# An RWKV recurrence with a cosine feed-forward on one core: block 1's own products earlier, its states later, the least value inside the scan, and weights' high parts on GpSimd

## The chip, the cores and the metric

The kernel runs on one core of a Trainium2 chip. The metric is the device time of one execution in microseconds, lower is better; the time shown is the median of the runs. In the text PE is TensorE, DVE is VectorE, ACT is ScalarE, POOL is GpSimd and SP is SyncE, which issues the DMAs.

## The reference

Per batch (4) and head (8), over 768 steps with 48 channels, a state of 48x48 decays by `w` and takes in `k v`; the output of all heads goes through a feed-forward of 384 to 2048 to 384 with `h*cos(h)`:

```python
for t in range(S):
    kt, vt, rt, wt = k[:, :, t], v[:, :, t], r[:, :, t], w[:, :, t]
    cur = np.einsum('bhd,bhe->bhde', u[None] * kt, vt)
    y[:, :, t] = np.einsum('bhd,bhde->bhe', rt, state + cur)
    state = wt[:, :, :, None] * state + np.einsum('bhd,bhe->bhde', kt, vt)
...
h = x @ w_in
g = h * np.cos(h)
return g @ w_out
```

## The kernel before, in words

The 3072 tokens are cut into 24 chunks of 128 tokens (4 batches, 6 chunks each), and two chunks make a block of 256 tokens. Chunk numbers `j` run through the batches first, so chunks 0 to 3 are the first of their batches and have no past state. The 2048 hidden channels are 16 weight tiles `w0` to `w15` of 128 channels, which stay in SBUF once they are prepared.

Attention of a chunk is a row of steps, named as in the tables that set the order:
- `load`, `lv`, `lr`: DMAs of `tt` (r, k and decays), `v`, and from chunk 8 on `rk`.
- `decay` (att_decay, L201): in the first eight chunks the product `rkt` (L205); a scan backwards over the decays into `ee` (L208), which gives the decay from each token to the end of the chunk; a lower bound on the whole decay (L212), its reciprocal (L213), a scan forwards (L214), and the scaled r (`r3`, L218) and k (`k3`, L219).
- `diag`: a product with `u` (a matmul `pc` in the first eight chunks, L230 to L233 on DVE after that), spread to a diagonal matrix `asb` by POOL (L237).
- `a`: scores `pa` on PE (L260), taken under a mask into `asb` by DVE (L262). `o` (L301): a block's own products `py` (L315, L320). `t`: transposed keys `kn`. `s`: states `pst` and `sn`. `d`: the decayed state `dd` and its copies `past`. `p` (L323): the products with the past (L330, L334), and the block's output `xT` split into a high and a low part.

The feed-forward of a block takes eight units of two weight tiles each. `mm1` (L383) makes `ph` in PSUM with three products per tile: high by high, high by low, low by high. The gate (L354) goes ACT L358, DVE L359, ACT L360, DVE L361, then ACT casts the high part `gs` (L141) and POOL subtracts it in two halves (L144) for the low part. `mm2` (L402) multiplies by the second matrix into `acc`. The first 16 units take turns between blocks 0 and 1 (`PAIR`), so that each weight tile serves twice while the next ones are prepared.

A weight tile arrives as packed bits (`raw`) and is rebuilt by `load_weights` (L153): three ACT passes (L163, L166, L167), a shift and an addition on DVE (L168, L169), the cast to the high part (`whi0`, a copy, L141: on ACT before) and the subtraction that gives the low part (`wlo0`, L144, on DVE).

What sets the order: the strings `START` (L61) and `PLAN` (L53) are PE's order, written out by hand ("w" prepares a weight tile and "f" fetches one, "m0 m1" are the halves of an mm1, a digit is a chunk or block). All other engines are ordered by a scheduling layer. `att` (L438) pulls in what a step needs, and forces older steps first where buffers run out. `EARLY` and `LATER` name the engine of each step: EARLY holds while START runs, which covers the attention of chunks 0 to 5, LATER from then on. The PSUM banks of `ph` are two while both blocks are under way, so an mm1 waits for the last gate step (L361) of the unit two before it.

```python
        if i < 2:
            stage[0] = 1 if i else 2
```

Of the kernel before, what the change touches and what calls it, by code (L numbers as in the profile page):

```python
# [17 lines left out]
ALU = mybir.AluOpType  # L18
# [19 lines left out]
LEAST = 1e-15  # L38
# [6 lines left out]

LAG = 3
HP = 50
EARLY = dict(rkt="v", cd="a", pc0="a", pc1="a", wadd="v", wm="a", whi0="a", whi1="a", ksh="a", gh="a", xh="a", rzh0="p", rzh1="v", r3="v", k3="v", rk="p", ru="p", rf0="v", rf1="v", kn="a", dd="v", rd0="a", rd1="a", rz0="v", rz1="v", ks="v", g0="p", g1="p", x="v", wlo0="v", wlo1="p", qf="s", qt="s", qr="s", qv="s", qx0="s", qx1="s", qo="s")
LATER = dict(pc0="a", pc1="a", ksh="v", gh="a", xh="a", rzh0="a", rzh1="a", r3="p", k3="v", rk="v", ru="v", rf0="v", rf1="v", kn="v", dd="v", rz0="v", rz1="v", ks="p", g0="p", g1="p", x="v", qf="s", qt="s", qr="s", qv="s", qx0="s", qx1="a", qo="s")
OFF = 0  # L50
FLEAD = 1
LEAD = 0
# [6 lines left out]
        "mm1 mm2 decay+5",  # L59
        "mm1 d+5 mm2 lr+6"]  # L60
START = ["load0 load1 f lv0 decay0 f diag0 a0 lv1 decay1 diag1 a1 w load2 f w o0 x0 decay2 diag2 m0 m1",  # L61
# [4 lines left out]
PAIR = "0001110101010101"  # L66
# [5 lines left out]
def rwkv_cos_ffn(ctx: ExitStack, tc: tile.TileContext, tr, tn, tv, u, ut, wts, w, rkw, vst, us, xs, out):  # L72
    nc = tc.nc
# [23 lines left out]
    def buf(tag, shape, dtype, name=None, pool=sb):  # L97
        return pool.tile(shape, dtype, tag=tag, name=name or tag, bufs=BUFS.get(tag, 1))
# [6 lines left out]
    mask = cst.tile([C, 4, C], U8, name="mask")  # L105
    nc.vector.tensor_copy(out=mask, in_=maskf)
    one_e = cst.tile([R, NP, 129], F32, name="one_e")
    nc.vector.memset(one_e, 0.0)
    nc.vector.memset(one_e[:, :, 128:129], 1.0)
    inj = cst.tile([R, NP, 129], F32, name="inj")  # L110
    nc.vector.memset(inj, 0.0)
# [5 lines left out]
    wholes = cst.tile([R, NG, NP], F32, name="wholes")  # L117
# [13 lines left out]
    def engines(codes):  # L131
        E.update({k: {"v": nc.vector, "p": nc.gpsimd, "a": nc.scalar, "s": nc.sync}[e] for k, e in codes.items()})
# [7 lines left out]
    def copy(name, out, in_):  # L140
        (nc.scalar.copy if E[name] is nc.scalar else E[name].tensor_copy)(out=out, in_=in_)  # L141
# [32 lines left out]
    NB = NG // NCB  # L174
# [4 lines left out]
    def att_load(j):  # L179
        a = atts[j] = {"j": j}  # L180
        a["g"] = g = order[j]
        a["b"], a["c"] = divmod(g, NCB)
        a["tt"] = tt = buf("tt", [R, TRW], F32)
        for cols in ((1024, TRW), (512, 1024), (0, 512)) if j < IN_PARTS else ((0, TRW),):
            E["qt"].dma_start(out=tt[:, slice(*cols)], in_=tr[g, :, slice(*cols)])
        a["r3"] = tt[:, 0:512].rearrange("p (a t) -> p a t", a=NP)
        a["k3"] = tt[:, 512:1024].rearrange("p (a t) -> p a t", a=NP)
        if j == 0:
            E["qt"].dma_start(out=u_by_head, in_=ut)
        if j == BY_PE:  # L190
            E["qt"].dma_start(out=u_sb, in_=u.to_broadcast([C, DM]))
# [9 lines left out]
    def att_decay(a):  # L201

        if a["j"] < BY_PE:
            a["rkt"] = buf("rkt", [R, NP, C], F32)
            E["rkt"].tensor_tensor(out=a["rkt"], in0=a["r3"], in1=a["k3"], op=ALU.mult)  # L205
        wp = a["tt"][:, 1024:1024 + W129 + 1]
        a["ee"] = ee = buf("ee", [R, NP, 129], F32)
        nc.vector.tensor_tensor_scan(out=ee.rearrange("p a t -> p (a t)")[:, ::-1], data0=wp[:, 1:W129 + 1][:, ::-1],  # L208
                                     data1=one_e.rearrange("p a t -> p (a t)")[:, ::-1],
                                     initial=0.0, op0=ALU.mult, op1=ALU.add)  # L210
        whole = wholes[:, a["j"]]
        nc.vector.tensor_single_scalar(out=whole, in_=ee[:, :, 0], scalar=LEAST, op=ALU.max)  # L212
        nc.vector.reciprocal(out=inj[:, :, 0], in_=whole)  # L213
        nc.vector.tensor_tensor_scan(out=wp[:, 0:W129], data0=wp[:, 0:W129], data1=inj.rearrange("p a t -> p (a t)"),  # L214
                                     initial=0.0, op0=ALU.mult, op1=ALU.add)
        pp = wp[:, 0:W129].rearrange("p (a t) -> p a t", a=NP)
        a["pp"] = pp[:, :, 0:C]
        E["r3"].tensor_tensor(out=a["r3"], in0=a["r3"], in1=a["pp"], op=ALU.mult)  # L218
        E["k3"].tensor_tensor(out=a["k3"], in0=a["k3"], in1=ee[:, :, 1:129], op=ALU.mult)  # L219
# [150 lines left out]
    def mm1(t, part=None):  # L370
        i, u = seq[t]
        if not part:
            weights("f", (u + 1) * FU + LEAD + FLEAD)
            weights("w", (u + 1) * FU + LEAD)
            for j in range(BLK):
                att(i * BLK + j, "x")
            units[t] = bank("h", [C, FU, BT], "ph")
        xT, ph = xts[i], units[t]
        for fi in range(FU) if part is None else (part,):
            n = 0  # L380
            for kt in range(KT):
                for a, b in PASSES:
                    nc.tensor.matmul(out=ph[:, fi], lhsT=wgt[u * FU + fi][:, 0, a, kt * 128:(kt + 1) * 128], rhs=xT[:, b, kt],  # L383
                                     start=n == 0, stop=n == 3 * KT - 1)
                    n += 1
        if part is None or part == FU - 1:
            units[t] = gate(sb, ph)
# [39 lines left out]
    for i in PAIR:  # L427
# [5 lines left out]
    n_checked = [0]  # L433
    done = {"f": 0, "w": 0}
    steps = dict(load=None, lr=att_load_rk, lv=att_load_v, decay=att_decay, diag=att_diag, d=att_dstate,
                 a=att_scores, t=att_transpose, s=att_state, o=att_own, p=att_past, x=att_x)

    def att(j, n):  # L438

        whole = n in "osp"  # L440
        if not 0 <= j < (NBLK if whole else NG) or (j, n) in seen:
            return
        for m in ("decay" if n == "diag" and j < BY_PE else NEEDS.get(n, "")).split():
            for c in (range(j * BLK, (j + 1) * BLK) if whole and m not in "osp" else (j,)):
                att(c, m)
        i = j // BLK
        if n == "load":
            for m in "osp":
                att((j - BUFS["tt"]) // BLK, m)
        elif n == "t":  # L450
            att((j - BUFS["kn"]) // BLK, "s")
        elif n == "d":
            att(i - SAME, "s")
            att((j - BUFS["dd"]) // BLK, "s")
            att(i - 1, "p")
        elif n == "lv":
            att((j - BUFS["v"]) // BLK, "o")
            att((j - BUFS["v"]) // BLK, "s")
        elif n == "x":
            att(i, "p")  # L460
        seen.add((j, n))
        if n == "load":
            att_load(j)
        else:
            steps[n](j if whole else atts[j])
# [19 lines left out]
    def events(i, row, t=None):  # L485
        for e in row.split():
            if e == "mm1":
                if t is not None:
                    up(0)
            elif e == "mm2":  # L490
                if t is not None and up1[1] <= t - LAG:
                    up(1)
            else:
                n, _, d = e.partition("+")
                att(i * (1 if n in "osp" else BLK) + int(d), n)
# [211 lines left out]
```

## Time and profile before

| | |
|---|---|
| time, median of 3 runs (lowest, highest) | 551.72 us (550.91, 552.66) |
| the profiled execution: own time, span | 554.87 us, 553.1 us |
| busy: PE, DVE, ACT, POOL | 517.9, 364.2, 270.5, 215.7 us |
| DMA | 51.38 MB, mean 93 GB/s |

Busy time is the union of an engine's instructions over the span, so a high share can hide a stage in which the engine waits. In the timeline a row has start, duration, engine, source line, operation, tiles with shapes and how many were merged; in brackets the idle time ahead of it and who ended it. A row of the waits has the total, the number of times and the longest. Start to start of two rows on PE is the better measure of a group of matmuls, since their ends overlap.

### The profile page before, as it was taken

The numbers are of one execution on the slowest core, as the hardware profiler recorded it, in microseconds if no ns is written. First come the engines' busy times: TensorE is split into PE (matmuls) and PEld (weight loads), VectorE is DVE, ScalarE is ACT, GpSimd is POOL, SyncE is SP. The second block draws the span as 40 slices with busy tenths as digits, with TensorE's granted clock in tenths as the row PEclk, the third lists the DMA queues.
The fourth block names the chain that finished last, engine by engine and source line by source line (L and its number), as shares of the span: only waits on it lengthen the run. The fifth ranks groups of instructions, "written<-read, shape, count | busy, mean of one in ns | idle before, by whom it ended". The sixth has DMA issues, their size and how long they took to land. (4 is left out here: it accounts for less than half of the span.)

```text
span 553.1 us, 11951 instructions
## 1 busy us (share of the span) xinstructions
PE 517.9 (94%) x4980; PEld 491.9 (89%) x4980; DVE 364.2 (66%) x574; ACT 270.5 (49%) x456; POOL 215.7 (39%) x268
## 2 busy tenths in 40 slices
PE   4656999989998999999999999999999999999996
PEld 3555999879998999999999999999999999999995
DVE  7999999955869468468468468468469674433321
ACT  1879998335424434434434435334443254444542
POOL 2151166623525335335335336335334334323332
PEclk9956899989999999999999999999999999999998
DMA  8985842005352043042042042043033340000000
GB/s 280 337 269 179 249 133 94 29 3 134 99 154 56 17 127 79 19 135 69 21 134 69 20 147 56 22 125 74 6 96 128 115 144 1 30 1 1 30 2 31
DMA packets 16440, 51.38 MB, mean 93 GB/s; under 512 B 1984, under 2 KB 8384, under 8 KB 16384
## 3 DMA queue, kind: packets, MB, share of 16 engines
q1 hardware_dynamic: 16240, 50.49, 30.2%
q8 instruction: 40, 0.66, 0.5%
q14 instruction: 16, 0.13, 0.1%
q10 hardware_dynamic: 144, 0.10, 0.1%
HBM read 45.87 MB, written 4.72 MB: 91 GB/s over the span
## 5 line engine op out<-in xcount | busy, mean ns | idle before, releaser
L144 POOL TENSOR_TENSOR gs<-rr,gs 128x256 fp32r<-128x256 f32 x192 | 156.2, 834 | 258.1 <-ACT gs L141 233.1
L383 PE MATMUL ph<-xT,w 128*128 128x256 f32 x1728 | 224.6, 285 | 6.4 <-DVE rr L361 3.5
L402 PE MATMUL acc<-w,gs 128*128 128x384 f32 x1152 | 222.1, 342 | 5.0 <-DVE asb L262 2.8
L383 PEld LDWEIGHTS ph<-xT,w 128*128 128x128 f32 x1728 | 215.5, 192 | 10.5 <-DVE w L144 2.9
L402 PEld LDWEIGHTS acc<-w,gs 128*128 128x128 f32 x1152 | 197.4, 190 | 11.0 <-DVE asb L262 3.5
L360 ACT ACTIVATE rr<-rr,quarter 128x512 f32<-128x512 f32 x96 | 69.5, 724 | 117.0 <-DVE rr L359 117.0
L359 DVE SCALAR_TENSOR_TENSOR rr<-rr,ph 128x512 f32<-128x512 int32 x96 | 65.6, 683 | 81.2 <-ACT rr L358 67.7
L361 DVE TENSOR_TENSOR rr<-rr,ph 128x512 f32<-128x512 f32 x96 | 65.3, 680 | 47.2 <-ACT rr L360 47.2
L358 ACT ACTIVATE rr<-ph 128x512 int32<-128x512 f32 x96 | 57.0, 593 | 57.0 <-PE ph L383 56.9
L141 ACT CAST gs<-rr 128x512 fp32r<-128x512 f32 x96 | 59.0, 615 | 51.7 <-PE acc L402 40.0
L237 POOL TENSOR_SCALAR_AFFINE_SELECT asb<-cd 128x512 f32<-128x512 f32 x48 | 34.3, 747 | 43.0 <-PE py L320 23.3
L262 DVE COPY_PREDICATED asb<-mask,pa 128x512 f32<-128x512 uint8 x48 | 32.7, 735 | 5.3 <-PE pa L260 5.3
L218 POOL TENSOR_TENSOR tt<-tt 112x512 f32<-112x512 f32 x18 | 23.6, 1309 | 28.3 <-DVE tt L214 27.1
L260 PE MATMUL pa<-tt 48*128 48x128 f32 x384 | 32.0, 311 | 2.3 <-DVE tt L219 2.2
L208 DVE TENSOR_TENSOR_SCAN ee<-tt,one_e 112x516 f32<-112x516 f32 x24 | 31.4, 1311 | 3.2 <-DMA tt<-tr 3.2
L260 PEld LDWEIGHTS pa<-tt 48*128 48x128 f32 x384 | 26.9, 210 | 7.4 <-issue 4.4
L214 DVE TENSOR_TENSOR_SCAN tt<-tt,inj 112x516 f32<-112x516 f32 x24 | 32.4, 1349 | 0.1
L141 ACT COPY past<-dd 48x192 f32<-48x192 f32 x40 | 14.0, 351 | 25.0 <-DVE dd L250 24.5
L225 PE MATMUL pc<-u_by_head,rkt 112*128 112x2 f32 x64 | 10.4, 285 | 13.4 <-DVE rkt L205 13.4
L225 PEld LDWEIGHTS pc<-u_by_head,rkt 112*128 112x128 f32 x64 | 10.3, 243 | 14.2 <-DVE rkt L205 7.9
L230 DVE TENSOR_TENSOR rk<-rk 128x384 f32<-128x384 f32 x16 | 10.9, 678 | 15.5 <-DMA rk<-tn 15.5
L219 DVE TENSOR_TENSOR tt<-tt,ee 112x512 f32<-112x512 f32 x24 | 19.8, 824 | 0.0
(66 smaller groups left out, 340.2 us busy)
## 6 DMA issues: line engine op xcount, KB each, us to landing
tt<-tr SPq DMA_DIRECT2D x22, 674.2 KB, 7.9
raw<-wts SPq DMA_DIRECT2D x16, 768.0 KB, 7.6
rk<-tn SPq DMA_DIRECT2D x16, 384.0 KB, 3.5
v<-tv SPq DMA_DIRECT2D x24, 224.0 KB, 7.0
ww<-w SPq DMA_DIRECT2D x6, 768.0 KB, 4.3
out<-ob SPq DMA_DIRECT2D x23, 192.0 KB, 2.0
tt<-tr SPq DMA_DIRECT2D x4, 224.0 KB, 4.3
tt<-tr SPq DMA_DIRECT2D x2, 226.2 KB, 3.6
```

Of the source, the lines that this page charges most:

```text
L141: (nc.scalar.copy if E[name] is nc.scalar else E[name].tensor_copy)(out=out, in_=in_)
L144: E[name].tensor_tensor(out=out, in0=full, in1=high.bitcast(F32), op=ALU.subtract)
L214: nc.vector.tensor_tensor_scan(out=wp[:, 0:W129], data0=wp[:, 0:W129], data1=inj.rearrange("p a t -> p (a t)"), initial=0.0, op0=ALU.mult, ...
L237: nc.gpsimd.affine_select(out=asb, in_=col.unsqueeze(2).to_broadcast([C, NP, C]), pattern=[[0, 4], [1, C]], compare_op=ALU.is_equal, fill= ...
L260: nc.tensor.matmul(out=pa[h][:, p], lhsT=a["k3"][rows(h), p], rhs=a["r3"][rows(h), p], start=True, stop=True)
L262: nc.vector.copy_predicated(a["asb", h], mask, pa[h])
L358: nc.scalar.activation(nn, ph, AF.Copy, scale=INV2PI / W_SCALE, bias=0.25)
L359: nc.vector.scalar_tensor_tensor(out=rr, in0=nn, scalar=-2.0 * math.pi * W_SCALE, in1=ph, op0=ALU.mult, op1=ALU.add)
L360: nc.scalar.activation(rr, rr, AF.Sin, scale=1.0 / W_SCALE, bias=quarter)
L361: nc.vector.tensor_tensor(out=rr, in0=rr, in1=ph, op=ALU.mult)
L383: nc.tensor.matmul(out=ph[:, fi], lhsT=wgt[u * FU + fi][:, 0, a, kt * 128:(kt + 1) * 128], rhs=xT[:, b, kt], start=n == 0, stop=n == 3 * K ...
L402: nc.tensor.matmul(out=accs[i][j][:, :DM], lhsT=gs[:, a, fi, j * C:(j + 1) * C], rhs=wgt[u * FU + fi][:, 1, b], start=u == 0 and fi == 0 a ...
```

## The change

- In START's second and third row, block 1's own products (`o1`) and `x2` move ahead of the first mm2; the third half-pair "m0 m1" (unit 2) and its weights come ahead of that mm2 too. The states (`t0 t1`, `s0`) of block 0 come later.
- The last scan into `ee` takes the maximum with a tile of the constant LEAST in place of adding zeros, so that the bound L212 goes away; `whole` is kept by a POOL copy for the check at the end.
- `whi0`: the high part of each of the 16 weight tiles is cast by POOL, before by ACT.
- `r3` in LATER (chunks 6 to 23): on DVE, before on POOL.
- The rule that pulls states in ahead of `d` no longer holds for the first four chunks.

```diff
-EARLY = dict(rkt="v", ... whi0="a", whi1="a", ...)
-LATER = dict(pc0="a", ... r3="p", ...)
+EARLY = dict(whole="p", rkt="v", ... whi0="p", whi1="p", ...)
+LATER = dict(whole="p", pc0="a", ... r3="v", ...)
...
-         "load3 f lv2 w f decay3 diag3 w m0 a2 m1 lv3 w f w a3 mm2 o1 x2 f",
-         "m0 m1 m0 m1 w f t0 t1 load4 mm2 s0 m0 m1 w f lv4 mm2 m0 m1 w f load5 lv5 mm2 t2 t3 m0 m1 w f s1",
+         "load3 f lv2 w f decay3 diag3 w m0 a2 m1 lv3 w f a3 o1 x2 w f m0 m1 mm2",
+         "m0 m1 w f t0 t1 load4 mm2 m0 m1 s0 w f lv4 mm2 m0 m1 w f load5 lv5 mm2 t2 t3 m0 m1 w f s1",
...
-    nc.vector.memset(one_e, 0.0)
+    nc.vector.memset(one_e, LEAST)
...
-                                     initial=0.0, op0=ALU.mult, op1=ALU.add)
-        whole = wholes[:, a["j"]]
-        nc.vector.tensor_single_scalar(out=whole, in_=ee[:, :, 0], scalar=LEAST, op=ALU.max)
-        nc.vector.reciprocal(out=inj[:, :, 0], in_=whole)
+                                     initial=0.0, op0=ALU.mult, op1=ALU.max)
+        nc.vector.reciprocal(out=inj[:, :, 0], in_=ee[:, :, 0])
+        copy("whole", wholes[:, a["j"]], ee[:, :, 0])
...
-        elif n == "d":
+        elif n == "d" and j >= NB:
```

Lines behind L211 have a number one lower in the changed kernel (L361 is L360 there, L218 is L217, L219 is L218).

How instructions move, at three places. First PE, behind the scores of chunk 3 (`pa` of the last row of L260 in START), before:

```order
L260 MATMUL pa<-tt 128x128 x8
L402 MATMUL acc<-w_181,gs 128x384 x2
L402 MATMUL acc<-w_195,gs 128x384 x2
...
L315 MATMUL py<-asb,v 32x128 x8
L320 MATMUL py<-asb,v 32x128 x8
...
L269 MATMUL pt<-ident,tt 128x112 x8
...
L383 MATMUL ph<-xT,w_382 128x256 x9
```

and now:

```order
L259 MATMUL pa<-tt 128x128 x8
L314 MATMUL py<-asb,v 32x128 x8
L319 MATMUL py<-asb,v 32x128 x8
...
L382 MATMUL ph<-xT,w_382 128x256 x9
L382 MATMUL ph<-xT,w_445 128x256 x9
L401 MATMUL acc<-w_181,gs 128x384 x2
L401 MATMUL acc<-w_195,gs 128x384 x2
...
L268 MATMUL pt<-ident,tt 128x112 x8
```

Block 1's own products (`py`) and unit 2's mm1 (tiles 4 and 5) stand ahead of unit 0's mm2 (`acc`); the transposes (`pt`) for block 0's states come later.

Second DVE, around the gates of units 10 to 12 (`rr_1003` with `ph_984`, `rr_1066` with `ph_1047`, `rr_1130` with `ph_1111`; `tt_1097` and `tt_1304` are chunks 6 and 7, `rk_1608` and `rk_1696` chunks 8 and 9), before:

```order
L361 TENSOR_TENSOR rr_1003<-rr_1003,ph_984 128x512
L231 TENSOR_TENSOR rk_1608<-rk_1608,u_sb_84 128x384
L230 TENSOR_TENSOR rk_1696<-rk_1696 128x384
L231 TENSOR_TENSOR rk_1696<-rk_1696,u_sb_84 128x384
L359 SCALAR_TENSOR_TENSOR rr_1066<-rr_1066,ph_1047 128x512
L262 COPY_PREDICATED asb_1031<-mask_75,pa_1085 128x512
L262 COPY_PREDICATED asb_1033<-mask_75,pa_1086 128x512
L361 TENSOR_TENSOR rr_1066<-rr_1066,ph_1047 128x512
L359 SCALAR_TENSOR_TENSOR rr_1130<-rr_1130,ph_1111 128x512
L361 TENSOR_TENSOR rr_1130<-rr_1130,ph_1111 128x512
```

and now:

```order
L360 TENSOR_TENSOR rr_1066<-rr_1066,ph_1047 128x512
L213 SCALAR_TENSOR_TENSOR tt_1097<-tt_1097,inj_80 112x516
L208 SCALAR_TENSOR_TENSOR ee_1416<-tt_1304,one_e_77 112x516
L217 TENSOR_TENSOR tt_1097<-tt_1097 112x512
L211 RECIPROCAL inj_80<-ee_1416 112x4
L218 TENSOR_TENSOR tt_1304<-tt_1304,ee_1416 112x512
L213 SCALAR_TENSOR_TENSOR tt_1304<-tt_1304,inj_80 112x516
L358 SCALAR_TENSOR_TENSOR rr_1130<-rr_1130,ph_1111 128x512
L217 TENSOR_TENSOR tt_1304<-tt_1304 112x512
L229 TENSOR_TENSOR rk_1608<-rk_1608 128x384
L360 TENSOR_TENSOR rr_1130<-rr_1130,ph_1111 128x512
```

The steps of chunks 6 and 7 that stood ahead of the gate of unit 11 stand behind it now, and ahead of the last step of the gate of unit 12; all but one product on `rk` come after that.

Third POOL, from the diagonals of chunk 2 on (`asb`; `gs` is a gate's pair), before:

```order
L237 AFFINE_SELECT asb<-cd 128x512 x6
L144 TENSOR_TENSOR gs<-rr,gs 128x256 x2
L237 AFFINE_SELECT asb<-cd 128x512 x2
L144 TENSOR_TENSOR gs<-rr,gs 128x256 x14
L237 AFFINE_SELECT asb<-cd 128x512 x2
```

and now:

```order
L141 CAST w_298<-h 128x2x384
L236 AFFINE_SELECT asb<-cd 128x512 x2
L141 COPY wholes<-ee 112x4
L144 TENSOR_TENSOR gs<-rr,gs 128x256 x2
L141 CAST w_330<-h 128x2x384
L141 CAST w_382<-h 128x2x384
L144 TENSOR_TENSOR gs<-rr,gs 128x256 x2
L141 CAST w_445<-h 128x2x384
L141 CAST w_527<-h 128x2x384
L141 CAST w_616<-h 128x2x384
L144 TENSOR_TENSOR gs<-rr,gs 128x256 x2
L141 CAST w_670<-h 128x2x384
```

A cast (`w`, 128x768) now stands between the pairs, in eight of the 16 cases directly behind one.

## Rows read from the trace of the kernel before

**Rows 1.** The page's first part: busy us, share of the span and number of instructions of each engine.

```profile
PE 517.9 (94%) x4980; PEld 491.9 (89%) x4980; DVE 364.2 (66%) x574; ACT 270.5 (49%) x456; POOL 215.7 (39%) x268
```

**Rows 2.** Busy time by stage: the stretch in us, its length, then busy time and number of instructions of PE, the weight loads, DVE, ACT and POOL, the granted share of PE's clock, the DMA share and GB/s.

```profile
30.00:50.00 20.00, 13.61 (x66) 11.99 (x67) 19.51 (x26) 16.69 (x23) 8.50 (x6) 0.50 0.63 202
50.00:70.00 20.00, 17.66 (x187) 16.59 (x187) 18.65 (x31) 19.62 (x29) 1.93 (x2) 0.88 0.79 235
70.00:90.00 20.00, 19.49 (x167) 19.04 (x166) 19.75 (x30) 19.26 (x30) 12.64 (x8) 1.00 0.43 129
90.00:110.00 20.00, 18.39 (x145) 17.26 (x144) 19.41 (x27) 10.54 (x19) 13.61 (x13) 1.00 0.13 45
200.00:500.00 300.00, 299.84 (x3045) 285.66 (x3044) 189.51 (x303) 129.17 (x233) 119.79 (x153) 1.00 0.25 74
```

**Rows 3.** PE's waits (total us, times, longest): the first two rows from 0 to 140 us, the last from 140 us to the end.

```profile
PE ph L383 <- DVE rr L361: 3.5, 3, 1.9
...
PE ph L383 <- DVE w L144: 2.4, 2, 1.7
...
PE acc L402 <- ACT gs L141: 1.3, 1, 1.3
```

**Rows 4.** PE's timeline, from 51 to 125 us (start, duration, engine, line, operation; idle time ahead in brackets).

```profile
51.41 0.64 PE L315 MATMUL py<-asb,v 128*32 128x128 f32 x16
...
53.30 0.60 PE L269 MATMUL pt<-ident,tt 112*128 112x112 f32 x4
...
65.96 2.26 PE L383 MATMUL ph<-xT,w 128*128 128x256 f32 x18
68.06 2.25 PE L402 MATMUL acc<-w,gs 128*128 128x384 f32 x12
70.15 2.26 PE L383 MATMUL ph<-xT,w 128*128 128x256 f32 x18
...
115.11 3.32 PE L383 MATMUL ph<-xT,w 128*128 128x256 f32 x18 [1.92 <-DVE rr L361]
...
120.69 0.61 PE L330 MATMUL py<-tt,past 112*32 112x128 f32 x16
...
121.83 2.37 PE L402 MATMUL acc<-w,gs 128*128 128x384 f32 x12
124.04 2.26 PE L383 MATMUL ph<-xT,w 128*128 128x256 f32 x18
```

**Rows 5.** DVE's timeline around the end of unit 11's gate.

```profile
111.99 0.56 DVE L231 TENSOR_TENSOR rk<-rk,u_sb 128x384 f32<-128x384 f32 x1
...
114.28 0.68 DVE L361 TENSOR_TENSOR rr<-rr,ph 128x512 f32<-128x512 f32 x1
```

**Rows 6.** The timeline of DVE and POOL from 78 to 90 us, and in the last two rows from 105 to 109 us.

```profile
78.64 0.15 DVE L212 TENSOR_SCALAR wholes<-ee 112x4 f32<-112x4 f32 x1
...
78.78 2.23 POOL L144 TENSOR_TENSOR gs<-rr,gs 128x256 fp32r<-128x256 f32 x2 [0.92 <-PE pst L287]
...
79.40 1.01 DVE L168 TENSOR_SCALAR h<-h 128x768 int32<-128x768 int32 x1
...
80.33 1.49 DVE L144 TENSOR_TENSOR w<-h,w 128x768 fp32r<-128x768 f32 x1
...
84.60 0.68 DVE L218 TENSOR_TENSOR tt<-tt 112x512 f32<-112x512 f32 x1
...
85.49 4.06 POOL L144 TENSOR_TENSOR gs<-rr,gs 128x256 fp32r<-128x256 f32 x2 [4.48 <-ACT gs L141]
...
86.07 0.55 DVE L168 TENSOR_SCALAR h<-h 128x768 int32<-128x768 int32 x1
86.54 0.68 DVE L359 SCALAR_TENSOR_TENSOR rr<-rr,ph 128x512 f32<-128x512 int32 x1
...
88.00 0.94 DVE L144 TENSOR_TENSOR w<-h,w 128x768 fp32r<-128x768 f32 x1
...
88.87 0.67 DVE L361 TENSOR_TENSOR rr<-rr,ph 128x512 f32<-128x512 f32 x1
...
105.52 1.00 DVE L219 TENSOR_TENSOR tt<-tt,ee 112x512 f32<-112x512 f32 x1
...
108.61 2.88 DVE L231 TENSOR_TENSOR rk<-rk,u_sb 128x384 f32<-128x384 f32 x1
```

**Rows 7.** Busy time by stage, columns as in rows 2.

```profile
116.00:120.00 4.00, 4.00 (x53) 3.69 (x55) 1.73 (x3) 2.03 (x4) 2.01 (x4) 0.57 0.02 4
```

**Rows 8.** Groups of instructions by line over the whole span: count, then busy us and mean ns of one, then the idle time ahead and what ended it.

```profile
L218 POOL TENSOR_TENSOR tt<-tt 112x512 f32<-112x512 f32 x18 | 23.6, 1309 | 28.3 <-DVE tt L214 27.1 <-DVE wholes L212 1.2
...
L141 ACT CAST w<-h 128x768 fp32r<-128x768 f32 x16 | 13.2, 826 | 0.9 <-DVE h L169 0.8
...
L103 POOL TENSOR_SCALAR_AFFINE_SELECT maskf<-maskf 128x512 f32<-128x512 f32 x1 | 0.6, 634 | 0.0
```

**Rows 9.** DVE's waits from 20 to 120 us (total us, times, longest).

```profile
DVE rr L359 <- ACT rr L358: 4.0, 4, 1.3
DVE h L168 <- ACT h L163: 0.8, 2, 0.6
```

**Rows 10.** The view of line 144 on POOL: duration in ns (least, median, most), first and last start.

```profile
L144 POOL TENSOR_TENSOR gs<-rr,gs x192: 725/738/2638, 31.8 to 545.0; 128x256 fp32r<-128x256 f32 x192
```

More of the change, by code (lines that the diff above doesn't have):

```diff
@@ L47 @@
 HP = 50
-EARLY = dict(rkt="v", cd="a", pc0="a", pc1="a", wadd="v", wm="a", whi0="a", whi1="a", ksh="a", gh="a", xh="a", rzh0="p", rzh1="v", r3="v", k3="v", rk="p", ru="p", rf0="v", rf1="v", kn="a", dd="v", rd0="a", rd1="a", rz0="v", rz1="v", ks="v", g0="p", g1="p", x="v", wlo0="v", wlo1="p", qf="s", qt="s", qr="s", qv="s", qx0="s", qx1="s", qo="s")
-LATER = dict(pc0="a", pc1="a", ksh="v", gh="a", xh="a", rzh0="a", rzh1="a", r3="p", k3="v", rk="v", ru="v", rf0="v", rf1="v", kn="v", dd="v", rz0="v", rz1="v", ks="p", g0="p", g1="p", x="v", qf="s", qt="s", qr="s", qv="s", qx0="s", qx1="a", qo="s")
+EARLY = dict(whole="p", rkt="v", cd="a", pc0="a", pc1="a", wadd="v", wm="a", whi0="p", whi1="p", ksh="a", gh="a", xh="a", rzh0="p", rzh1="v", r3="v", k3="v", rk="p", ru="p", rf0="v", rf1="v", kn="a", dd="v", rd0="a", rd1="a", rz0="v", rz1="v", ks="v", g0="p", g1="p", x="v", wlo0="v", wlo1="p", qf="s", qt="s", qr="s", qv="s", qx0="s", qx1="s", qo="s")
+LATER = dict(whole="p", pc0="a", pc1="a", ksh="v", gh="a", xh="a", rzh0="a", rzh1="a", r3="v", k3="v", rk="v", ru="v", rf0="v", rf1="v", kn="v", dd="v", rz0="v", rz1="v", ks="p", g0="p", g1="p", x="v", qf="s", qt="s", qr="s", qv="s", qx0="s", qx1="a", qo="s")
 OFF = 0
```

## The prediction

> **What bounds the kernel now.** I read the page first: TensorE (PE) is busy for 94% of the span, VectorE (DVE) for 66% [rows 1]. That is a mean over unlike stages, so the table by stage comes next [rows 2]: from 200 to 500 us PE is busy for 299.84 of 300 us, and from 140 us on the one wait of any length takes 1.3 us [rows 3]. Nothing that another engine saves there can show. In the first 130 us it is otherwise: from 30 to 110 us DVE is busy for 19.4 to 19.8 of every 20 us, except 18.65 in one window, and from 50 to 90 us ScalarE (ACT) is full as well (19.6 and 19.3). So what can move is the start: the span is the time that PE loses there, plus a fixed amount of matmul work.
>
> Where does PE lose it last? The PE waits before 140 us [rows 3] and the PE timeline [rows 4] say: for weights early on, and later 3.5 us in three waits for L361, the last DVE step of a gate. The wait of 1.92 us at 115.11 us is the last one. Number the pairs mm1/mm2 in PE's order as units 0, 1, 2: this mm1 is unit 13's; it takes over the PSUM bank of unit 11 (ph_1047), which L361 of unit 11 sets free at 114.28 + 0.68 = 114.96 us [rows 5]. DVE has hardly stood still until then. **DVE's work in front of the binding gate sets the end**, and the sum is made there.
>
> **The change, part by part.**
>
> *Order.* In DVE's order some 160 instructions stand in front of the end of unit 11's gate before. In the changed kernel that gate stands further forward; steps of chunks 6 to 8 come behind it, in front of the last step of the gate of unit 12. Up to there DVE has the same instructions as before up to unit 11, except: one more gate (L359 and L361, 0.68 each: +1.36), two more products L218, of chunks 6 and 7 (they were GpSimd's, POOL's; 0.68 each: +1.36), eight L212 fewer (0.15 undisturbed: -1.2) and three products on `rk` fewer (0.56 each: -1.7) [rows 5, 6]. Sum -0.2 us: DVE is there at the same moment as before. But the gate of unit 12 frees the bank of unit 14, and PE's mm1 of unit 14 stands one mm1 (65.96 to 68.06: 2.10), block 2's own products (as 51.41 to 53.30: 1.89), its past products (120.69 to 121.83: 1.14) and one mm2 (68.06 to 70.15: 2.09) behind that of unit 13 [rows 4]: 7.2 us. Term: **-7.4 us**. The earlier own products of block 1 are no second gain: they let PE do its rows sooner, and then it waits for DVE at the later gate. From 115.11 to 124.04 us PE really took 8.93 us for that 7.2, partly at the lower of its two clocks (1.2 of 2.4 GHz; granted 0.57 from 116 to 120 us, after idle time [rows 7]). I expect the same gaps again and count nothing, with 1.7 us for the range.
>
> *r3 of chunks 6 to 23 from POOL to DVE.* POOL gives up 18 products of 1309 ns [rows 8], DVE gains 18 of 0.68: 12 us. Sixteen lie where PE does not wait (DVE is busy for 189.5 of 300 us there [rows 2]): nothing. Two lie between 104 and 110 us, and around them DVE's own steps grew: L219 took 1.00 instead of the 0.68 of its like, L231 2.88 instead of 0.56 [rows 5, 6]: 2.6 us, in part the doing of POOL's other steps. With the two gone from POOL: **-2.0 us**, ends 0 and -2.6.
>
> *ACT loses the 16 casts of high parts* (826 ns each [rows 8], 13.2 us). DVE waits for ACT 4.0 us in its gates between 20 and 120 us (four waits, the longest of 1.3 us, not all of them ahead of the binding gate) and 0.8 us in its shifts [rows 9]. Of these 4.8 us: **-1.0 us**, ends 0 and -2.4 (half of them).
>
> *POOL gains 16 casts of 128x768.* No row shows a cast on POOL. A one-input step of 128x512 takes 634 ns undisturbed (L103) [rows 8]; scaled by size that is 0.95 us, a little less if part of it is fixed: taken as 0.92 us. The two-input products give the far end, 1.31 x 768/512 = 1.96. GPSIMD Engine Reference, section 3.1, of the Trainium skill gives 1.03 to 1.8 cycles per element for one input; an estimate by it would be 0.66 to 1.15 us, with which the sum below would lie between -5.4 and +0.7, and no run here shows it yet.
>
> What matters is not POOL's time but what it does to DVE, and the timeline of both has the picture [rows 6]. POOL's pair for a gate's low part, 1.48 us at twice the median of 738 ns [rows 10], took 4.06 us at 85.49 us beside a DVE that read two SBUF tiles almost without a break; it came through when L359 and L361 ran, which read one input from PSUM. And at 79.40 us such a pair stretched DVE's L168 from 0.55 to 1.01 and its weight subtraction from 0.94 to 1.49: 1.01 us for 1.48 us of POOL. So a cast is free only beside a DVE step that reads PSUM (0.68 us), and then sticks out by 0.92 - 0.68 = 0.24. By DVE's order between a weight's addition (L169) and its subtraction, five of the 16 (weights 1, 4, 6, 7, 14) have such a step for themselves: 5 x 0.24 = 1.2. For weights 0 and 2 there is none, and for the other nine a gate's pair stands ahead of the cast in POOL's row (once with two diagonals behind it) and uses it up. These eleven I price at the share just seen, 1.01/1.48 of 0.92 = 0.63: 6.9. Term: **+8.1 us**, ends 16 x 0.24 = 3.8 and 16 x 0.92 = 14.7.
>
> *The rest.* `whole` becomes a POOL copy of 112x4, no larger than L212; it would count only if the scan two chunks later had to wait for it to let go of `ee`. The maximum in the scan leaves the scan's length. On SP's queue two weight fetches pass the load of chunk 4, and two `v` loads fall behind one fetch: DVE's backlog covers both. The order behind unit 15 stays.
>
> Sum: -7.4 - 2.0 - 1.0 + 8.1 = **-2.3 us**. The profiled execution took 554.87 us (span 553.1), 3.15 above the median 551.72 of the runs; it would become 552.6, and the median **549.4 us**.
>
> **Rivals.** (1) *Slower: POOL blocks DVE outright.* If each of the 16 casts costs DVE its full 0.92 us, because cast and subtraction follow directly on one another and POOL gets several queued steps in ahead of DVE (as in the 2.88 us of L231), the sum is -10.4 + 14.7 = +4.3: 556.0. It decides from 0.65 us per cast on (10.4/16). For it: DVE is full in just that stage, and a pair precedes the cast nine times. Against: a DVE that waits for a cast leaves POOL alone, so POOL's queue clears. SBUF — State Buffer, section "SBUF: two separate sides", of the Trainium skill makes this a rule: a GpSimd step and a DVE step with two SBUF inputs share one pair of ports, whoever starts first holds it for the whole instruction, and the other is blocked. The stretched rows agree with a hold, but they also show DVE running several such steps in succession while POOL waits; how often POOL gets in first no row tells. (2) *Covered casts:* each sticks out 0.24 us: -10.4 + 3.8 = -6.6, 545.1. For it: POOL is busy for 1.9 us of 20 between 50 and 70 us. Against: for 12.6 of 20 in the next window, most of it in waiting [rows 2]. (3) *The change does not reach the end:* weights 3 and 5, whose casts stand behind a pair, come 1.48 + 0.92 = 2.4 us later, early in the stage, and everything behind them shifts by as much: -2.3 + 2.4, no change, 551.8. For it: unit 1's second half waits 1.7 us for a weight already [rows 3].
>
> **How the numbers follow.** No change means within 0.3% (1.65 us), about what a measurement of this kernel can tell. Forecast 0.45 (547 to 551.5); rival 1 0.25; rival 2 0.17; rival 3 0.13. Two thirds of the forecast's case and all of rival 2 are faster by more than 0.3%: with rounding 0.48. The rest of the forecast's case and most of rival 3 make 0.26; rival 1 and a remainder 0.26. The range takes in rival 2 and nearly all of rival 1, with the unknown price of the cast: 545.0 to 555.5. As cases of both signs hold most of the chance, the forecast's own range stands beside it, 547 to 551.5.
>
> **What would show it.** Right: PE's last wait for a gate is that for unit 12, near 120 us; mm1 of unit 14 starts near 121.7 instead of 124.04 us; casts on POOL take 0.9 to 2 us, DVE's L168, L169 and scans are stretched beside them, and DVE waits for POOL in front of its subtractions; ACT is far from full between 50 and 90 us. Wrong: longer PE waits near 60 us than now, casts of over 2 us in the mean, or PE waits behind 140 us.

## The result, and the profile after

| | before | changed |
|---|---|---|
| time, median of 7 runs (lowest, highest) | 551.59 us (550.70, 552.66) | 554.84 us (553.74, 556.45) |
| ratio, 95% interval | | 1.0061 (1.0045, 1.0077) |
| the profiled execution: own time, span | 554.87 us, 553.1 us | 555.0 us, 552.9 us |

The changed kernel is slower by 0.61%, 3.3 us, where 2.3 us less was forecast. The two profiled executions are equally long, but that of before lies 3.3 us above its median and that of after at its own. A second execution of before (below) took 552.45 us, span 550.7; that is the one to compare with, and rows called "before again" are from it.

First the shares, as in [rows 1], and the stages, columns as in [rows 2]:

```profile
PE 518.1 (94%) x4980; PEld 494.1 (89%) x4980; DVE 369.2 (67%) x568; ACT 260.4 (47%) x440; POOL 220.3 (40%) x290
```

```profile
30.00:50.00 20.00, 12.60 (x123) 10.50 (x124) 16.35 (x24) 16.18 (x21) 9.28 (x11) 0.66 0.60 187
50.00:70.00 20.00, 17.19 (x147) 16.33 (x145) 18.38 (x24) 18.40 (x26) 10.14 (x11) 1.00 0.63 205
70.00:90.00 20.00, 18.06 (x150) 17.29 (x151) 16.84 (x27) 14.74 (x22) 11.80 (x10) 1.00 0.53 135
90.00:110.00 20.00, 17.35 (x128) 16.65 (x129) 19.14 (x24) 10.85 (x21) 15.14 (x14) 0.91 0.25 80
148.00:156.00 8.00, 6.57 (x37) 6.23 (x36) 3.89 (x7) 2.35 (x6) 2.61 (x4) 0.57 0.50 150
200.00:500.00 300.00, 300.00 (x3087) 286.63 (x3078) 191.92 (x305) 128.81 (x234) 109.58 (x156) 1.00 0.25 74
```

ACT is no longer full from 50 to 90 us, but DVE is not full either (16.84 of 20 against 19.75): it has begun to wait. And there is a stretch at 148 to 156 us, in none of the stages that the prediction looked at, in which PE is busy for 6.57 of 8 us at a granted clock of 0.57; before again it is busy for 8.00 there at 1.00.

PE's waits (columns as in [rows 3]), the first four from 0 to 140 us, the last from 140 us on; and DVE's largest from 20 to 125 us:

```profile
PE ph L382 <- POOL w L141: 6.1, 3, 4.5
PE pc L224 <- DVE asb L261: 2.6, 1, 2.6
PE ph L382 <- DVE rr L360: 1.8, 2, 1.5
...
PE pt L268 <- DVE xT L144: 1.2, 1, 1.2
...
PE pa L259 <- ACT ob L414: 1.4, 1, 1.4
```

```profile
DVE w L144 <- POOL w L141: 8.9, 9, 1.9
```

Last PE's timeline, columns as in [rows 4]:

```profile
114.65 2.26 PE L382 MATMUL ph<-xT,w 128*128 128x256 f32 x18
...
122.40 2.34 PE L382 MATMUL ph<-xT,w 128*128 128x256 f32 x18 [0.27 <-DVE rr L360]
124.58 2.25 PE L401 MATMUL acc<-w,gs 128*128 128x384 f32 x12
128.06 1.13 PE L268 MATMUL pt<-ident,tt 112*128 112x112 f32 x8 [1.23 <-DVE xT L144]
...
144.67 2.25 PE L401 MATMUL acc<-w,gs 128*128 128x384 f32 x12
...
149.55 2.07 PE L259 MATMUL pa<-tt 48*128 48x128 f32 x14 [1.43 <-ACT ob L414]
151.55 6.41 PE L382 MATMUL ph<-xT,w 128*128 128x256 f32 x36
157.89 0.64 PE L314 MATMUL py<-asb,v 128*32 128x128 f32 x16
```

The mm1 of unit 14 (122.40 us) starts 1.64 us earlier than in [rows 4] and waits for the gate of unit 12, as forecast, though for 0.27 us only. At 128.06 us the lead is gone: the transposes wait 1.23 us for an `xT`, while before again they start at 128.05 without a wait. Then comes the new wait at 149.55 us for the PSUM bank of chunk 9's scores, and behind it 36 matmuls take 6.41 us; before again the same 36 take 4.47 us, from 148.53 us on. That stretch alone, from the mm2 at 144.67 to the `py` at 157.89 us, is 13.22 us long against 8.46 (144.48 to 152.94).

### The profile page after: what moved, and what is told of

It reads as the page before. It is cut to its first block, busy times and chain, and to the rows that moved or that the text cites. A ratio compares the mean times of both kernels' runs of the same rounds, so it can differ in the third digit from the quotient of the medians.

```text
span 552.9 us, 11929 instructions
## 1 busy us (share of the span) xinstructions
PE 518.1 (94%) x4980; PEld 494.1 (89%) x4980; DVE 369.2 (67%) x568; ACT 260.4 (47%) x440; POOL 220.3 (40%) x290
## 5 line engine op out<-in xcount | busy, mean ns | idle before, releaser
L144 POOL TENSOR_TENSOR gs<-rr,gs 128x256 fp32r<-128x256 f32 x192 | 160.2, 856 | 216.4 <-ACT gs L141 205.8
L359 ACT ACTIVATE rr<-rr,quarter 128x512 f32<-128x512 f32 x96 | 69.4, 723 | 115.3 <-DVE rr L358 114.9
L358 DVE SCALAR_TENSOR_TENSOR rr<-rr,ph 128x512 f32<-128x512 int32 x96 | 65.5, 682 | 77.6 <-ACT rr L357 64.7
L360 DVE TENSOR_TENSOR rr<-rr,ph 128x512 f32<-128x512 f32 x96 | 65.4, 682 | 44.6 <-ACT rr L359 44.6
L236 POOL TENSOR_SCALAR_AFFINE_SELECT asb<-cd 128x512 f32<-128x512 f32 x48 | 35.7, 775 | 38.2 <-PE py L319 25.9
L261 DVE COPY_PREDICATED asb<-mask,pa 128x512 f32<-128x512 uint8 x48 | 32.9, 734 | 5.4 <-PE pa L259 5.4
L259 PE MATMUL pa<-tt 48*128 48x128 f32 x384 | 33.4, 316 | 1.6 <-ACT ob L414 1.4
L141 POOL COPY wholes<-ee 112x4 f32<-112x4 f32 x24 | 8.3, 345 | 57.1 <-DVE ee L208 57.1
L213 DVE TENSOR_TENSOR_SCAN tt<-tt,inj 112x516 f32<-112x516 f32 x24 | 30.2, 1259 | 0.1
L144 DVE TENSOR_TENSOR w<-h,w 128x768 fp32r<-128x768 f32 x16 | 16.6, 1038 | 9.0 <-POOL w L141 8.9
L141 POOL CAST w<-h 128x768 fp32r<-128x768 f32 x16 | 14.8, 927 | 14.3 <-DVE h L169 14.3
```

The costliest lines, as they stand in the source:

```text
L144: E[name].tensor_tensor(out=out, in0=full, in1=high.bitcast(F32), op=ALU.subtract)
L236: nc.gpsimd.affine_select(out=asb, in_=col.unsqueeze(2).to_broadcast([C, NP, C]), pattern=[[0, 4], [1, C]], compare_op=ALU.is_equal, fill= ...
L259: nc.tensor.matmul(out=pa[h][:, p], lhsT=a["k3"][rows(h), p], rhs=a["r3"][rows(h), p], start=True, stop=True)
L261: nc.vector.copy_predicated(a["asb", h], mask, pa[h])
L358: nc.vector.scalar_tensor_tensor(out=rr, in0=nn, scalar=-2.0 * math.pi * W_SCALE, in1=ph, op0=ALU.mult, op1=ALU.add)
L359: nc.scalar.activation(rr, rr, AF.Sin, scale=1.0 / W_SCALE, bias=quarter)
```

## The experiments

Each time is the median of its runs, each ratio is to the kernel before on the same chip, where its medians were 551.6 to 552.6 us; so rows are compared by their ratios, and differences in us below are worked out from these.

| run | what it is | us | ratio (95%) |
|---|---|---|---|
| changed | | 554.84 | 1.0061 (1.0045, 1.0077) |
| e1_casts_back | changed, casts on ACT | 546.77 | 0.9896 (0.9876, 0.9916) |
| e2_casts_alone | before, casts on POOL | 556.99 | 1.0068 (1.0042, 1.0094) |
| e3_order_back | changed, old order | 556.89 | 1.0084 (1.0058, 1.0110) |
| e4_r3_back | changed, r3 on POOL | 554.54 | 1.0049 (1.0026, 1.0072) |
| e8_casts_r3_back | order and maximum alone | 545.71 | 0.9881 (0.9847, 0.9916) |
| e6_order_alone | before, new order | 544.91 | 0.9869 (0.9835, 0.9904) |
| e9_spare_casts | e1 with unread casts into rd | 553.74 | 1.0027 (1.0002, 1.0052) |
| e12_spare_u8 | e1 with unread casts to bytes | 550.05 | 0.9952 (0.9930, 0.9974) |
| e13_seven_casts | changed, 7 casts on POOL, 9 on ACT | 547.92 | 0.9915 (0.9888, 0.9943) |
| e10_r3_back_89 | changed, r3 of chunks 8, 9 on POOL | 552.34 | 0.9988 (0.9967, 1.0009) |
| e11_casts_r3_89 | e1 and e10 together | 543.77 | 0.9838 (0.9816, 0.9861) |

### Before once more

No edit.

> The kernel before, unchanged, for a second profiled execution. If the first one (own time 554.87 us, 3.15 above the median of its runs) was an unusual execution, this one should take 551 to 552.5 us, and it should show where the 3 us were: by the lower clock around 56 to 64 or 116 to 120 us, or by DVE's steps stretched beside POOL's. If the profile itself costs 3 us, it takes 554 to 555.5 again.

It took 552.45 us: the first profile was an unusual execution. The two stand within 0.2 us of one another at 158 us; by 410 us the first is 1.4 us behind, and the end behind PE's last matmul is 0.9 us longer. The lower clock at 116 us is in both (0.53 and 0.50 from 116 to 118 us). That near 60 us is in the first alone (0.53 from 58 to 60 us, 1.00 in the second, which has 0.50 and 0.59 from 50 to 54 us instead), and it is not what made the difference, as the two are level at 158 us. To subtract the profile's offset from the sum was right.

### The parts taken back: casts, order

```diff
 e1_casts_back (from the changed kernel), the reverse in e2_casts_alone (from before)
-EARLY = dict(... whi0="p", whi1="p", ...)
+EARLY = dict(... whi0="a", whi1="a", ...)
 e3_order_back: START and the rule for "d" as before; e6_order_alone: the reverse, from before
```

> The changed kernel with the 16 high parts cast by ACT again; all else as in the changed kernel. Theory A (the casts on POOL eat the gain: in the changed kernel PE waits 6.1 us for them ahead of 140 us and DVE 8.9 us): 554.8 less a good part of 6.1, so 547 to 550, faster than the kernel before. Rival B (the new order loses by itself, and the casts cost little): 553.5 to 555, still slower than before. Rival C (nothing before 140 us reaches the end; the loss comes later, with r3 on DVE): 554 to 555.5, and the wait of 1.4 us for the scores' bank at 149.5 us is still there.

> The kernel before with one edit, the 16 high parts cast by POOL. Theory A: slower than before by 4 to 8 us (the sum priced the casts at +8.1 less 1.0 for ACT's relief), so 555.5 to 559.5. Rival B: within 1.5 us of before, 550.5 to 553. Rival C: as rival B.

> The changed kernel with START and the rule for the states as before; casts on POOL, the maximum in the scan and r3 on DVE stay. Theory A: slower than the changed kernel, since the gain of the order (7.4 us by the sum) is lost while the casts' cost stays: 558 to 562. Rival B: 551 to 552.5, as fast as before. Rival C: 554 to 555.5.

> The kernel before with the new START and the rule for the states alone. If the order is the whole gain (term of -7.4 us): 544 to 546, as with the order and the maximum together, with PE's unit 14 some 8 us earlier than before. If the maximum in the scan carries a part of it (eight steps L212 of 0.15 us fewer ahead of the gate, and one step less between the two scans): 1 us or more above that.

Theory A holds in the main: with the casts on ACT the kernel is 1.04% faster than before, and 1.65% (9.1 us) faster than the changed one (546.77 us, just under the range). Put into the kernel before, the casts cost 0.68% (3.8 us); DVE waits for them 5.5 us there, in five waits, instead of 8.9 in nine. The order alone is worth 1.31% (7.2 us), the term's 7.4; the maximum adds nothing that can be seen (e8 beside e6). With the casts on POOL the order is worth only 0.23% (the intervals of the two overlap): e3 took 556.89 us, below the 558 to 562 of Theory A and above the ranges of both rivals. So the parts do not add up. The casts cost 5.3 us less in the old order, and half of that lies ahead of the binding gate: in the old order the casts delay unit 11's by 4.3 us (it ends at 119.28 us in e2 and at 114.96 before), in the new order unit 12's by 7.1 (below). Why was not tried.

In the kernel with the casts on ACT, DVE's gate of unit 12 and PE's mm1 of unit 14 and next transposes are:

```profile
114.47 0.68 DVE L360 TENSOR_TENSOR rr<-rr,ph 128x512 f32<-128x512 f32 x1
```

```profile
115.41 2.26 PE L382 MATMUL ph<-xT,w 128*128 128x256 f32 x18
...
120.32 1.13 PE L268 MATMUL pt<-ident,tt 112*128 112x112 f32 x8 [0.56 <-DVE xT L144]
```

The gate ends at 115.15 us, where that of unit 11 ended before (114.96 in [rows 5]): as the order's term forecast, DVE is there at about the same moment, one unit further (the r3 term would have it there 2.0 us earlier). In the changed kernel it ends at 122.26 us:

```profile
121.58 0.68 DVE L360 TENSOR_TENSOR rr<-rr,ph 128x512 f32<-128x512 f32 x1
```

So the casts cost DVE 7.11 us up to there. From its first instruction on, DVE stands idle for 12.9 us up to that point instead of 6.1, which is 6.8 of the 7.1; its busy time grows by only 0.3 us (with one product on `rk` of 0.55 us fewer ahead of the gate). How the cost splits differs between executions: e10 (below) has the same rows on PE, DVE, ACT and POOL up to 140 us, but there the gate ends at 122.80 us, with 5.5 us more idle time and 2.2 us more busy time than in e1, and DVE waits for casts for 6.3 us instead of 8.9. Most of the cost is idle time in both. The timeline of DVE and POOL in the changed kernel shows one such wait:

```profile
84.06 3.15 POOL L144 TENSOR_TENSOR gs<-rr,gs 128x256 fp32r<-128x256 f32 x2 [2.77 <-ACT gs L141]
84.40 0.93 DVE L169 CUSTOM_DVE_ANT_0 h<-h,rd 128x1536 uint16<-128x1536 uint16 x1
...
87.15 0.19 POOL L141 COPY wholes<-ee 112x4 f32<-112x4 f32 x1
87.28 0.83 POOL L141 CAST w<-h 128x768 fp32r<-128x768 f32 x1
88.15 0.96 DVE L144 TENSOR_TENSOR w<-h,w 128x768 fp32r<-128x768 f32 x1 [1.54 <-POOL w L141]
```

The addition L169 is done at 85.33 us, but POOL is in a gate's pair until 87.21, then does a copy, then the cast; DVE's subtraction is next in DVE's row and waits, and the gate behind it with it.

### Which casts cost, and is it the wait?

```diff
 e13_seven_casts (from the changed kernel)
-copy("whi%d" % kind, high, hf)
+(copy("whi%d" % kind, high, hf) if f in (0, 1, 2, 4, 6, 7, 14) else nc.scalar.copy(out=high, in_=hf))
 e9_spare_casts (from e1); e12_spare_u8 writes into a byte tile `spare` of its own in place of rd
+nc.gpsimd.tensor_copy(out=rest_of.bitcast(F32R), in_=hf)
 low_part("wlo%d" % kind, rest, hf, high)
```

> The changed kernel with the casts of weights 0, 1, 2, 4, 6, 7 and 14 on POOL and those of the nine weights whose cast stands behind a gate's pair in POOL's row on ACT. By the prediction's prices (nine times 0.63 us, less some of ACT's relief): 554.8 less 5.2, so 549 to 550.5. By DVE's waits in the changed kernel (6.1 of its 8.1 us before the gate of unit 12 stand before subtractions of those nine): 547.5 to 549.5. If what counts is POOL's time beside DVE and not the place in its row: seven sixteenths of the loss of 8 stay, 550.5 to 551.5.

> The changed kernel with the 16 high parts cast by ACT, and POOL besides casting each into a tile that nobody reads (the spent rd), at the place in its row where its own cast stood. POOL has the same work as in the changed kernel, but DVE does not wait for it. Theory W (what costs is that DVE's subtraction waits for a cast that stands behind other steps in POOL's row): 546 to 548.5, near the 546.8 without casts. Rival S (POOL's casts slow DVE through shared access to SBUF, waited for or not): 551 to 555.

> As the kernel with spare casts, but each is written as bytes into a tile of its own, so that ACT need not wait for POOL to let go of rd (4.7 us of such waits there). Nobody waits for these casts but through h. If what they cost is DVE's steps stretched beside POOL's (4.3 us more DVE time up to the gate of unit 12 in that run): 550 to 552.5. If it was ACT's wait for rd: 546.5 to 548.5.

With the seven casts alone DVE waits once for a cast (0.7 us), and the gate of unit 12 ends at 116.22 us, 1.07 later than with none on POOL:

```profile
DVE w L144 <- POOL w L141: 0.7, 1, 0.7
```

```profile
115.55 0.67 DVE L360 TENSOR_TENSOR rr<-rr,ph 128x512 f32<-128x512 f32 x1
```

So the nine casts behind a pair make up 6.04 of the 7.11 us, 0.67 each; the prediction had 0.63. (Weight 14's cast stands behind a pair too, but DVE does not wait for it. DVE's single waits for the nine add up to 6.4 us in the changed kernel; the expectation has 6.1.) As the gate of the same rows can differ by 0.5 us between executions, 6.04 is no sharper than that. By the times the nine cost 1.46% (8.1 us) and the seven 0.19% (1.0 us).

That it is the wait alone is refuted. e9 came close to the changed kernel though nobody waits for its casts; but there ACT waited 4.7 us for POOL to let go of `rd`, so it settles little. e12 has not that fault, and still 0.56% (3.1 us) of the 1.65% remain. Its gate of unit 12 ends at 118.85 us, 3.7 late, with only 0.6 us more idle time: now it is DVE's own steps that are longer, by 3.1 us. (The kernel of e12 has two lines more: L145, L169, L170, L219 and L238 there are L144, L168, L169, L217 and L236 of the changed kernel.)

```profile
87.20 0.68 DVE L219 TENSOR_TENSOR tt<-tt 112x512 f32<-112x512 f32 x1
87.22 2.08 POOL L173 CAST spare<-h 128x768 uint8<-128x768 f32 x1
87.80 0.55 DVE L169 TENSOR_SCALAR h<-h 128x768 int32<-128x768 int32 x1
...
91.67 1.69 POOL L238 TENSOR_SCALAR_AFFINE_SELECT asb<-cd 128x512 f32<-128x512 f32 x2
...
92.80 1.37 DVE L145 TENSOR_TENSOR w<-h,w 128x768 fp32r<-128x768 f32 x1
93.31 1.54 POOL L173 CAST spare<-h 128x768 uint8<-128x768 f32 x1
94.09 1.57 DVE L170 CUSTOM_DVE_ANT_0 h<-h,rd 128x1536 uint16<-128x1536 uint16 x1
```

At 87 us DVE is first, keeps its undisturbed times, and the cast takes 2.08 us. At 93 us POOL is first: the subtraction starts while two diagonals run (until 93.36 us) and takes 1.37 us instead of 0.95, the cast behind it takes 1.54 beside the subtraction, and the addition starts beside the cast and takes 1.57 instead of 0.94. The Trainium skill (SBUF — State Buffer, "SBUF: two separate sides") says that of a GpSimd step and a DVE step with two SBUF inputs the one that starts first holds a shared pair of ports for its whole instruction. The rows agree as to who is late; but a cast that always blocked DVE would cost 0.8 us and more, and in e12 sixteen of them cost 3.7, or 0.23 each.

### r3 on DVE

```diff
 e4_r3_back (from the changed kernel), e8_casts_r3_back (from e1)
-LATER = dict(... r3="v", ...)
+LATER = dict(... r3="p", ...)
 e10_r3_back_89 (from the changed kernel), e11_casts_r3_89 (from e1)
-E["r3"].tensor_tensor(out=a["r3"], ...)
+(nc.gpsimd if a["j"] in (8, 9) else E["r3"]).tensor_tensor(out=a["r3"], ...)
```

> The changed kernel with r3 of chunks 6 to 23 on POOL again. Theory D (r3 on DVE is what costs: two L217 and a scan stand ahead of the gate's L358 at 147.7 us, ACT's copy of the output L414 stands behind that gate, the scores' bank comes free 1.4 us late at 149.5 us, and the clock falls behind it): the wait and the lower clock are gone, 551 to 553 us. The prediction's term (r3 off POOL is worth 2.0 us ahead of the gate of unit 12): slower than the changed kernel, 556.5 to 558.

> The changed kernel with the casts on ACT and r3 on POOL again, so the order and the maximum in the scan alone. Theory D: faster than with the casts alone undone (546.8), by 1.5 to 3.5 us: 543.5 to 545.5. The prediction's term: slower than that one, 548 to 549.5.

> The changed kernel with r3 of chunks 8 and 9 alone on POOL again; PE's and ACT's orders stay as they are, and r3 of chunks 6 and 7 stays on DVE. Theory D (those two steps cause the wait of 1.4 us for the scores' bank at 149.5 us and the lower clock behind it; r3 of chunks 6 and 7 off POOL is worth 2 us ahead of the gate of unit 12): no wait at 149.5, 3 to 4 us faster than the changed kernel, 550.5 to 552. Rival (that wait only moves to another place, as the kernel with r3 wholly back on POOL suggests, which took 554.5): 554 to 555.

> The same edit with the casts on ACT besides. Theory D: 543 to 545, some 2 to 3 us below the 546.8 of the casts alone undone. Rival: 546 to 547.

The time of e4 tells neither theory: it has no wait at 149 us, but its gate of unit 12 ends at 124.46 us, 2.2 later. No cast runs there any more; POOL takes 2.55 us for the r3 of chunk 6 from 116.24 us on, and DVE's steps beside it grow, the L218 at 117.75 us to 2.28 from 0.66 and the scan behind it to 1.76 from 1.22. (0.67 of the 2.2 us are there at the gate of unit 11 already, ahead of the first row that differs.) So the prediction's -2.0 holds at its place. At PE's last matmul e4 is 2.7 us ahead of the changed kernel, by the times only 0.12%, less than the intervals; in its profile the stretch behind that matmul is 5.7 us long instead of 4.0. e8 is no clearer (0.15% under e1, less than the intervals). e10 separates the two: with r3 of chunks 8 and 9 alone on POOL, the kernel is 0.73% (4.0 us) faster than the changed one (552.34 us, 0.3 above Theory D's range and 1.7 below the rival's). PE's and ACT's orders are untouched; on DVE a mask step L261 and a reciprocal L211 move forward besides. Here is DVE and ACT in the changed kernel, ahead of the wait:

```profile
140.13 1.06 DVE L217 TENSOR_TENSOR tt<-tt 112x512 f32<-112x512 f32 x1
...
144.18 1.17 DVE L218 TENSOR_TENSOR tt<-tt,ee 112x512 f32<-112x512 f32 x1
145.27 1.77 DVE L213 TENSOR_TENSOR_SCAN tt<-tt,inj 112x516 f32<-112x516 f32 x1
147.08 0.69 DVE L217 TENSOR_TENSOR tt<-tt 112x512 f32<-112x512 f32 x1
147.69 0.68 DVE L358 SCALAR_TENSOR_TENSOR rr<-rr,ph 128x512 f32<-128x512 int32 x1
148.40 0.72 ACT L359 ACTIVATE rr<-rr,quarter 128x512 f32<-128x512 f32 x1 [2.92 <-DVE rr L358]
149.03 0.85 ACT L414 ACTIVATE ob<-acc 128x384 f32<-128x384 f32 x2
```

and with r3 of chunks 8 and 9 on POOL:

```profile
144.26 1.21 DVE L213 TENSOR_TENSOR_SCAN tt<-tt,inj 112x516 f32<-112x516 f32 x1
...
145.39 0.66 DVE L218 TENSOR_TENSOR tt<-tt,ee 112x512 f32<-112x512 f32 x1
...
145.55 1.55 POOL L217 TENSOR_TENSOR tt<-tt 112x512 f32<-112x512 f32 x1 [2.15 <-DVE tt L213]
146.06 0.69 DVE L358 SCALAR_TENSOR_TENSOR rr<-rr,ph 128x512 f32<-128x512 int32 x1
146.78 0.72 ACT L359 ACTIVATE rr<-rr,quarter 128x512 f32<-128x512 f32 x1 [0.75 <-DVE rr L358]
...
147.41 0.85 ACT L414 ACTIVATE ob<-acc 128x384 f32<-128x384 f32 x2
...
148.19 1.16 PE L259 MATMUL pa<-tt 48*128 48x128 f32 x16
```

Two L217 (1.06 and 0.69 us) stand ahead of the gate's step L358 on DVE, and L218 and the scan L213 take 0.5 us more each. The step runs at 147.69 instead of 146.06 us, although PE is 0.55 us further on in the changed kernel. ACT keeps its order: the cosine L359 waits for L358, and `ob`, which copies an output from PSUM and so frees the bank for the scores, stands behind L359. With chunk 9's r3 on POOL `ob` comes in time; from the mm2 (145.22) to the `py` (153.68) it is 8.46 us again, 4.76 less. In this kernel the stretch is, columns as in [rows 2]:

```profile
148.00:156.00 8.00, 8.00 (x121) 7.53 (x121) 5.85 (x12) 2.75 (x6) 4.46 (x8) 1.00 0.52 150
```

With the casts on ACT as well, 543.77 us, as Theory D had it: 1.6% faster than before, the best of all.

## Why the prediction was wrong

**What bounds: right.** The end of the start is set by DVE's work in front of a gate, and PE's last wait for a gate is that for unit 12, at 122.40 us. (In e1, without the casts, PE does not wait there at all.)

**Order, -7.4: right in the time.** Alone it is worth 7.2 us. DVE's sum of -0.2 in it is not borne out. In e6 the gate of unit 12 has one more gate ahead of it and nothing less (+1.36 by the sum) and ends 0.5 to 0.7 us later than that of unit 11 (115.42 us in e6; 114.96 before, 114.76 before again). The eight L212 that the maximum saves were to be worth -1.2; with them gone, in e8, that gate ends 0.68 us later still (116.10).

**r3 of chunks 6 and 7, -2.0: right there** with POOL's casts in the kernel (1.5 to 2.2, from e4 and the changed kernel); without them it is 0.95 (116.10 in e8, 115.15 in e1). In both pairs the two L217 on DVE take the place of two products on `rk`, which the sum prices at +0.24 net.

**Casts +8.1, ACT's relief -1.0: right in size at the gate**, 7.11 for a net 7.1 (no run takes the two apart), and in how it falls on the two kinds of cast: 6.04 for the nine where 5.7 was said, 1.07 for the seven where 2.5 was. The cast itself took 927 ns in the mean where 0.92 was said; the second row has the least, the median and the most in ns:

```profile
L141 POOL CAST w<-h 128x768 fp32r<-128x768 f32 x16 | 14.8, 927 | 14.3 <-DVE h L169 14.3
```

```profile
L141 POOL CAST w<-h x16: 819/832/1155, 18.4 to 105.0; 128x768 fp32r<-128x768 f32 x16
```

Mean and median lie in the estimate of 0.66 to 1.15 us which follows from the GPSIMD Engine Reference, section 3.1, of the Trainium skill: the trace agrees.

The picture behind it was half right. The price was derived from steps stretched beside POOL; in the changed kernel nearly all of it is DVE standing still for a cast late in POOL's row (5.5 of 7.7 us in e10), and the stretching shows where DVE does not wait (e12). Rival 1's price, 0.92 for each, did not come; that its time, 556.0, is nearer to the measured one than the forecast is luck. Nor did rival 3: PE waits 4.50 us for weight 3's cast at 40.69 us, but with the cast on ACT it waits 5.85 for it at 39.48, and by 49.7 us the two kernels are level.

At the end of the kernel the casts cost 9.1 us by the times, 2 more than at the gate. PE's rows in the changed kernel and in e1 show where: the mm1 of unit 14 is 6.99 us later, the transposes behind it 7.74 (the wait for `xT` takes 1.23 us instead of 0.56), and from the `py` behind the scores of chunk 9 on PE is 9.02 us later, to its last matmul, as the stretch from the mm2 to the `py` takes 13.22 us instead of 11.93. In e1 that stretch is:

```profile
141.82 1.16 PE L259 MATMUL pa<-tt 48*128 48x128 f32 x14 [1.43 <-ACT ob L414]
...
148.87 0.65 PE L314 MATMUL py<-asb,v 128*32 128x128 f32 x16
```

A wait of PE for `asb` at 100.31 us (2.65 us, the second row of the waits above; 0.52 in e1), behind which an mm2 takes 3.87 us instead of 2.33, stands ahead of the gate and is part of the 6.99.

**At the gate the sum was about right, in part by luck.** The mm1 of unit 14 was forecast 2.3 us earlier, near 121.7 us; it starts at 122.40, 1.64 earlier. Two errors nearly cancel in this. DVE's terms say that the gate of unit 12 ends 4.9 us later than that of unit 11 before (-0.2 - 2.0 - 1.0 + 8.1); it ends 7.3 later (122.26 against 114.96), the L212 being the largest part of the difference. But the 1.7 us that PE lost before behind its wait at 115 us, partly at the lower clock, were expected again and did not come: the mm1 of unit 13 takes 2.26 us now instead of 3.32.

**What failed is the step "Sixteen lie where PE does not wait: nothing".** It read the room for r3 of chunks 8 to 23 from 200 to 500 us, where DVE is busy for 189.5 of 300 us, and that is true there: PE is busy for 300.00 of 300 in the changed kernel. But chunks 8 and 9 come at 140 to 148 us, in none of the stages read. From 136 to 148 us DVE was busy for 11.2 of 12 us before; with two more products for 11.97. The row "PE waits behind 140 us", named as a sign of being wrong, is what came: 4.76 us in one place. e10 takes it away and the kernel is level with before. The whole adds up so: the change without its casts and without r3 of chunks 8 and 9 (e11) is worth -8.9 us where the sum had -9.4, the casts (e10 against e11) +8.3 where it had 7.1, and r3 of chunks 8 and 9 (the changed kernel against e10) +4.0 where it had nothing. So this step is 4.0 of the 5.6 us between the forecast and the result, and the casts, too cheap behind the gate, are 1.2.

**What is left.** Against before again, at the same rows of PE: -1.46 at the mm1 of unit 14, +1.67 by 133 us for the most part at the late `xT`, +4.74 by 163 us at the scores' bank, -2.14 by 205 us, all of it from 172 to 181 us, where two waits of before (1.1 and 0.2 us, in and ahead of one mm2) do not occur: +2.8 together, near the 3.3 of the times. The wait for `xT` and the two that went were not tried by themselves.

## What to carry to other kernels

An off-loaded step costs by its place more than by its duration: if the next instruction of the full engine needs it, ask what stands ahead of it in the other engine's row, and if nothing waits for it, it can still stretch the full engine's steps (0.23 us for each cast in e12). Work given to an engine that is "two thirds busy" has to be placed at its first occurrence, in the stage where the engine still catches up; then follow whoever waits for the step behind it, through engines that keep their order, down to the buffer that is freed last. And take the parts of a change apart before judging it: here one part gained 7 us and two others lost it all and 3 us more.

## What the runs showed of the hardware

A wait of 1.43 us cost 4.76. PE had just run eight matmuls of two columns (`pc`) and two of the scores; after the wait the granted clock in that stretch was 0.57 (so partly 1.2 of 2.4 GHz), and the rest of the scores took 2.07 us instead of 1.16 and the 36 matmuls behind them 6.41 instead of 4.47. The same wait cost 3.47 in e1, where the scores still ran in 1.16 us and the 36 matmuls took 6.03. Before, a wait of 1.1 us at 175 us between full matmuls left the clock at 1.00.

The stretch from PE's last matmul to the end is 4.0 to 5.7 us long and differs between kernels and between two executions of the same one (5.5 and 4.6 for before); what sets it was not looked for, and differences of a microsecond in single spans should not be read as effects. Nor is a wait in one execution exact: with the same rows DVE waited for casts for 8.9 us in one execution and for 6.3 in another, and the same gate ended 0.5 us apart.
